# Later chunks convolved a step sooner and transposed by the DMA crossbar, no adds of x in the steps where chunks enter

## The chip, the cores and the metric

The kernel runs on one core of a Trainium2 chip. The metric is the device time of one execution in microseconds (us). A kernel was executed several times; the numbers below are medians with lowest and highest, and one execution of each kernel left a profile and a trace. Engines are called as the profile calls them: PE (tensor engine), DVE (vector), ACT (scalar), POOL (GpSimd), SP (sync); a "q" after the name (ACTq) is that engine's stream of DMA issues.

## The reference

A causal convolution of 7 taps over the sequence gives x; then a phase layer mixes tokens with two 4224x4224 matrices and channels with two 192x192 ones.

```python
def _attn_ref(x, weight):                  # x: 8 x 4224 x 192, weight: 8 heads x 7 taps
    w = softmax(weight)                    # (cut) over the taps, + 1e-9 in the divisor
    out = np.einsum('hk,bskhg->bshg', w, windows(x))        # causal, zero padded
    return out.reshape(B, S, D)

def _moe_ref(x, w_theta, w_tok_r, w_tok_i, w_ch):
    theta = x @ w_theta
    zr, zi = x * np.cos(theta), x * np.sin(theta)
    y = np.einsum('ts,bsd->btd', w_tok_r, zr) + np.einsum('ts,bsd->btd', w_tok_i, zi)
    u = x + y
    return u + np.maximum(u @ w_ch, 0.0)
```

Nearly all the work is the two token mixes, a product of 4224x4224 by 4224x1536 twice. The kernel does them by a scheme of seven products instead of eight for each pair of blocks.

## The kernel before

The 4224 tokens are cut into 33 **chunks** of 128. A chunk is loaded, convolved on PE, transposed, multiplied with w_theta, and turned into seven operands `z`. Eleven chunks fit in SBUF at a time. The output rows are 33 blocks, worked on in pairs: a **step** is one pair of row blocks against the chunks present, seven **runs** of up to 22 matmuls (a step with one block has four). After 17 steps a chunk has met all rows, and its place goes to the next. So there are 58 steps, and three kinds:

- **entering steps** 17 to 22 and 35 to 40, in which chunks 11 to 32 replace older ones, mostly two in a step;
- **quiet steps** 23 to 34, with eleven chunks and nothing else;
- **final steps** 41 to 57, which also compute the output; for it u is transposed by 24 DMA crossings.

```python
base = [0, 0, 1, 1, 2, 3, 3, 4, 4, 5, 5]
start = [base[k % NW] + (NU + 1) * (k // NW) for k in range(NK)]   # NW = 11, NU = 17
...
def crossed(uT, u):                                   # 128 x 1536, 384 KB, issued by ACT
    act(nc.scalar.dma_start(out=uT, in_=u, transpose=True))

def transposed(uT, u, by_dve=False):                  # 6 transposes on PE, then a copy
    tp = banks("tp", F16)
    for k in range(6):
        pe(nc.tensor.transpose(tp[:, 0, k * P : (k + 1) * P], u[:, k * P : (k + 1) * P], ident))
    evacuate(uT.rearrange("p k s -> p (k s)"), tp[:, 0, 0 : 6 * P], by_dve)
...
class Chunk:
    def conv(self, j):
        if j == 0:
            self.z = zpool.tile([P, 7, HN], F16, name="z", tag="z")
            self.x = self.z[:, T2 : T2 + 2, :].rearrange("p t n -> p (t n)")   # x lies inside z
        ...                                           # 8 matmuls, ACT copies; j == 1 writes xs
    def tasks(self):
        for j in range(2):
            yield lambda j=j: self.conv(j)
        for g in range(NG):
            yield lambda g=g: self.transpose(g)       # transposed(...), one half each
        for g in range(NG):
            yield lambda g=g: self.theta(g)
        ...                                           # products (DVE), differences (DVE)
```

Every row block must have x added once. An **add of x** is done in one of two ways. In most steps POOL adds `xr`, read back from DRAM, to the partial sums `pv`. For steps called `ahead`, x is added in DRAM by an accumulating DMA of two halves, some steps before the sums are read.

```python
visits = [v for v in range(NU, NSTEP) if v % NU == t % NU]
for i, tb in enumerate(self.tbs):
    at = [v for v in visits if self.known(tb) < v - 1 and v + NU < NSTEP]
    at = at[0] if at else visits[-1]
    if t == at:
        self.adds.append(i)
...
def add_x(self, i):
    if not self.ahead:
        xr = wk.tile([P, N], F16, name="xr", tag="xr", bufs=1)
        nc.sync.dma_start(out=xr, in_=xs[rows, :])
        pool(nc.gpsimd.tensor_tensor(out=self.pv[i], in0=self.pv[i], in1=xr, op=ALU.add))
        return
    for cols in (slice(0, HN), slice(HN, N)):
        pool(nc.gpsimd.dma_start(out=part[...][self.tbs[i], :, cols],
                                 in_=xs[rows, cols], accum_op=ALU.add))
```

Work is hung into a step by its position from 0 to 7: loads of weights two steps ahead, the turning of weights on DVE one step ahead, chunk loads at 4.5 of the step two before a chunk's start, everything else of a chunk from 0.1 on in the step before its start.

Of the kernel before, what the change touches and what calls it, by code (L numbers as in the profile page):

```python
# [16 lines left out]
def kernel(  # L17
# [91 lines left out]
    def banks(name, dtype=F32):  # L109
        return mmpool.tile([P, 2, PC if dtype == F32 else 2 * PC], dtype,  # L110
                           name=name, tag="mm")
# [20 lines left out]
    def channel_mix(tT, w):  # L132

        v = banks("v")
        for k in range(2):
            for b in range(2):
                for i in range(2):
                    pe(nc.tensor.matmul(  # L138
                        v[:, k, b * D : (b + 1) * D], lhsT=tT[:, 3 * k + b + i, :],
                        rhs=w[:, 2 * b + i, :], start=(i == 0), stop=(i == 1),  # L140
                    ))
        return v[:, :, 0 : 2 * D]
# [24 lines left out]
    class Chunk:  # L167
# [23 lines left out]

        def conv(self, j):

            if j == 0:
                self.z = zpool.tile([P, 7, HN], F16, name="z", tag="z")
                self.x = self.z[:, T2 : T2 + 2, :].rearrange("p t n -> p (t n)")
            pc = banks("pc")
            for h in range(4):
                for half in range(2):
                    pe(nc.tensor.matmul(  # L200
                        pc[half * 2 * Q : (half + 1) * 2 * Q, h // 2,
                           h % 2 * B * G : (h % 2 + 1) * B * G],
                        lhsT=bands[:, 4 * j + h, :, :].rearrange("p a m -> p (a m)"),
                        rhs=self.xw[:, half, :, (4 * j + h) * G : (4 * j + h + 1) * G],
                        start=True, stop=True,
                    ))
            evacuate(
                self.x.rearrange("p (b d) -> p b d", d=D)[
                    :, :, 4 * j * G : 4 * (j + 1) * G
                ].rearrange("p b (i h g) -> p i h b g", i=2, h=2),  # L210
                pc[:, :, 0 : 2 * B * G].rearrange("p i (h b g) -> p i h b g", h=2, b=B),
                self.k == 0 and j == 1,
            )
            if j == 1:
                for a in range(NQ):
                    t0 = token(self.k, a)
                    nc.sync.dma_start(
                        out=xs[t0 : t0 + Q, :], in_=self.x[a * Q : (a + 1) * Q, :]
                    )

        def transpose(self, g):
# [4 lines left out]
                0 < self.k < 3 or (self.k, g) == (0, 1),  # L226
            )

        def theta(self, g):
            v = channel_mix(self.xT[:, 6 * g : 6 * g + 6, :], wth).rearrange(  # L230
                "p k (b h e) -> p k b h e", b=2, h=2
            )
            for first, bias in ((Z11, half_pi[:]), (Z21, None)):
                o = self.z[:, first : first + 2, :].rearrange(
                    "p h (k b e) -> p k b h e", b=2, e=HD
                )[:, 2 * g : 2 * g + 2, :, :, :]
                args = dict(out=o, in_=v, func=AT.Sin)
                if bias is not None:
                    args.update(bias=bias, scale=1.0)
                act(nc.scalar.activation(**args))  # L240
# [14 lines left out]
        def tasks(self):  # L255

            for j in range(2):
                yield lambda j=j: self.conv(j)
            for g in range(NG):
                yield lambda g=g: self.transpose(g)  # L260
            for g in range(NG):
                yield lambda g=g: self.theta(g)
            yield lambda: self.product(Z11)
            yield lambda: self.product(Z21)
            yield lambda: self.sums(0)
            yield lambda: self.sums(1)
# [13 lines left out]
    class Step:  # L280


        def __init__(self, t):
            self.t, self.u, self.ks = t, unit(t), active(t)
            self.n = len(self.ks)
            self.tbs = [tb for tb in (2 * self.u, 2 * self.u + 1) if tb < NT]
            self.pair = len(self.tbs) == 2
            self.first = t < NU
            self.final = t + NU >= NSTEP
            self.late = self.final and self.n < NW  # L290
            self.ahead = self.late or 0 <= t + NU - NSTEP < 2
            visits = [v for v in range(NU, NSTEP) if v % NU == t % NU]
            self.adds = []
            for i, tb in enumerate(self.tbs):
                at = [v for v in visits if self.known(tb) < v - 1 and v + NU < NSTEP]
                at = at[0] if at else visits[-1]
                if t == at:
                    self.adds.append(i)
            self.time = 0.324 * self.n * (7 if self.pair else 4)
            self.st, self.w, self.ub, self.uT, self.pv = {}, {}, {}, {}, []  # L300
# [199 lines left out]
    def step_events(t):  # L500
        found = []
        s = steps[t]
        if t + 1 < NSTEP:
            found += steps[t + 1].w_tasks()
            found.append((1.6, steps[t + 1].load_rows))
            if not steps[t + 1].ahead:
                for i in steps[t + 1].adds:
                    found.append((3.3 + 1.7 * i, lambda i=i: steps[t + 1].add_x(i)))
        for s in steps[t:]:
            if s.ahead and t == s.t - (4 if s.late else 10):  # L510
                for i in s.adds:
                    found.append((3.3 + 1.7 * i, lambda s=s, i=i: s.add_x(i)))
        if t + 2 < NSTEP:
            nxt = steps[t + 2]
            for m in (1, 2):
                found.append((1.3 + 3 * (m - 1), lambda m=m: nxt.load_w(m)))
        for at, f in outputs:
            begin = at - sum(s.time for s in steps[:t])
            if 0 <= begin < steps[t].time:
                found.append((7 * begin / steps[t].time, f))  # L520
        if t >= NU - 2:
            new = [k for k in range(NK) if start[k] == t + 2 and k >= NW]
            for k in new:
                found.append((4.5, lambda k=k: load_chunk(k)))
            at = 0.1
            for k in (k for k in range(NK) if start[k] == t + 1 and k >= NW):
                pos = [0, .5, 1.3, 1.6, 2.1, 2.5, 3.1, 3.15, 3.4, 3.6]

                def add(at, j, k):
                    def go():  # L530
                        if j == 0:
                            chunks[k].todo = chunks[k].tasks()
                        next(chunks[k].todo)()
                    found.append((at, go))
                for j, p in enumerate(pos):
                    add(at + p, j, k)
                at += 2.3
        return found


# [185 lines left out]
```

## Time and profile before

| | before |
|---|---|
| time | 1475.88 us median of 3 (1469.09 to 1477.83), profiled execution 1468.28 |
| PE busy | 1418.6 of 1466.6 us, mean granted clock 0.999 |
| transposes of x on PE in later rounds | 44 groups of six, 0.33 us each |
| adds of x | 30 on POOL, 6 accumulating transfers |
| crossings | 24, all in final steps |

The page and the timeline are read in the prediction below. The page's DMA queues: each line gives packets, MB, and the time that the packets took as a share of what 16 engines have in the span; the crossings are queue 10.

```profile
q10 hardware_dynamic: 37632, 9.44, 3.8%
```

All instructions on the tile `uT` in the kernel before: for the issue of a crossing the shortest, median and longest time in ns, and in the last line the time from issue to landing in us.

```profile
L155 ACTq DMA_TRANSPOSE uT<-ub x24: 1290/1436/4943, 1065.0 to 1376.0; - x24
...
DMA to landing us min/median/max: 3.2/6.2/10.0
```

Last the DMA view of the first entering steps alone, 410 to 565 us: the two large queues, and of two transfers the KB and the median time to landing.

```profile
q0 software_dynamic: 22724, 10.49, 55.2%
q1 hardware_dynamic: 6320, 22.42, 41.3%
...
xs<-z SPq DMA_DIRECT2D x36, 96.0 KB, 4.0
st<-in_moe_w_tok_i_dram POOLq DMA_DIRECT2D x16, 144.0 KB, 4.7
```

A packet of a crossing is 9.44 MB / 37632 = 251 bytes on average, and 24 crossings took 3.8% x 1466.6 / 24 = 2.3 us of all engines each. And in the entering steps, where the change puts 22 more, the queues already stand at 55.2 + 41.3 = 97%, though nothing is late yet.

### The profile page before, as it was taken

Reading aid. Unit: us, or ns where it says so; the run is one execution under the profiler, and the core shown is the slowest. Engines: PE = TensorE matmul, PEld = TensorE weight load, DVE = VectorE, ACT = ScalarE, POOL = GpSimd, SP = SyncE. Lnnn points to the kernel's source line nnn. Section 1 sums busy time; section 2 is a strip of 40 time slices with the busy share of each in tenths; the row PEclk is TensorE's granted clock in tenths of the full one; section 3 lists DMA queues with packets and bytes.
Section 4 is the critical chain, followed back from the end, with each engine's and each line's share of the span. In section 5 each row is a group of like instructions: output and inputs, shape, how many; then the busy total and the mean of one; then the engine's idle time right before and its main releaser. Section 6 shows DMA issues by size and latency. Waiting matters only on the chain.

```text
span 1466.6 us, 23784 instructions
## 1 busy us (share of the span) xinstructions
PE 1418.6 (97%) x9807; PEld 887.2 (60%) x9807; DVE 1021.4 (70%) x1050; ACT 323.1 (22%) x413; POOL 444.7 (30%) x649
## 2 busy tenths in 40 slices
PE   7789999999999899999999999989999999999997
PEld 4556666666666466666656556656666666666665
DVE  6884554545548777866776767877878777767676
ACT  6861111111124145000000003434210010010034
POOL 7422211111233432341422442443224124213210
PEclk9999999999999999999999999999999999999999
DMA  9976756465699999987886899989979989999983
GB/s 172 219 174 147 139 98 151 89 150 97 138 232 213 201 259 222 242 221 188 196 222 148 240 162 217 254 198 228 241 165 219 206 198 219 200 216 204 213 208 123
DMA packets 271165, 279.63 MB, mean 191 GB/s; under 512 B 106576, under 2 KB 240080, under 8 KB 271056
## 3 DMA queue, kind: packets, MB, share of 16 engines
q0 software_dynamic: 160736, 87.43, 46.9%
q1 hardware_dynamic: 72688, 181.24, 35.5%
q10 hardware_dynamic: 37632, 9.44, 3.8%
q8 instruction: 77, 1.26, 0.3%
q14 instruction: 32, 0.26, 0.1%
HBM read 245.49 MB, written 103.42 MB: 238 GB/s over the span
## 4 chain that ended last, share of the span: by engine, by line
PE 84%; DVE 8%; ACT 3%; DMA 2%; issue 1%; POOL 1%; DVEq 0%; SPq 0%; ACTq 0%; POOLq 0%
PE y L426 76%; PE v L138 5%; DVE wt L338 2%; DVE pv L391 2%; ACT z L240 2%; PE pc L200 2%; PE tp L160 1%; DVE z L245 1%; DMA uT<-ub 1%; DVE z L251 1%; DVE wt L326 1%; ACT uT L148 1%; DVE pv L463 1%; ACT pv L389 0%; POOL pv L373 0%
## 5 line engine op out<-in xcount | busy, mean ns | idle before, releaser
L426 PE MATMUL y<-z,wt 128*128 128x384 f16 x7656 | 1290.1, 326 | 20.5 <-DVE pv L391 19.5
L426 PEld LDWEIGHTS <-wt 128*128 128x128 f16 x7656 | 739.9, 98 | 495.9 <-issue 22.1
L391 DVE TENSOR_TENSOR pv<-y,pv 128x768 f32<-128x768 f32 x324 | 308.4, 952 | 307.5 <-PE y L426 260.7
L326 DVE STREAM_TRANSPOSE wt<-st 128x1408 f16<-128x1408 f16 (+7 forms) x224 | 327.5, 1464 | 40.4 <-PE y L426 36.2
L313 POOL DMA_DIRECT2D st<-in_moe_w_tok_i_dram x232 | 132.5, 580 | 486.8 <-DVE wt L326 463.9
L313 POOL DMA_DIRECT2D st<-in_moe_w_tok_r_dram x232 | 132.7, 581 | 458.5 <-DVE wt L326 445.2
L338 DVE TENSOR_TENSOR wt<-wt 128x1408 f16<-128x1408 f16 (+7 forms) x216 | 219.4, 1016 | 45.6 <-PE y L426 43.4
L148 ACT ACTIVATE z<-pc 128x768 f16<-128x768 f32 x65 | 52.9, 813 | 400.5 <-PE pc L200 400.5
L448 ACT ACTIVATE ub<-pv 128x768 f16<-128x768 f32 x66 | 52.5, 835 | 342.4 <-DVE pv L391 337.3
L389 ACT ACTIVATE pv<-y 128x768 f32<-128x768 f32 x66 | 53.7, 813 | 282.7 <-PE y L426 282.7
L138 PEld LDWEIGHTS <-uT 128*128 128x128 f16 x1056 | 90.8, 98 | 25.9 <-issue 7.8
L373 POOL TENSOR_TENSOR pv<-pv,xr 128x1536 f32<-128x1536 f32 x30 | 94.5, 3151 | 15.5 <-issue 8.1
L187 POOL DMA_DIRECT2D xw<-in_x_dram x132 | 76.7, 596 | 25.8 <-issue 7.0
L463 DVE SCALAR_TENSOR_TENSOR pv<-v,pv 128x768 f32<-128x768 f32 x66 | 62.8, 954 | 22.4 <-PE v L138 20.2
L148 ACT ACTIVATE uT<-tp 128x768 f16<-128x768 f16 x79 | 63.0, 815 | 63.1 <-PE tp L160 62.2
L251 DVE TENSOR_TENSOR z<-z 128x768 f16<-128x768 f16 x132 | 73.3, 555 | 3.8
L245 DVE TENSOR_TENSOR z<-z 128x1536 f16<-128x1536 f16 x66 | 63.5, 997 | 9.0 <-ACT z L240 9.0
L240 ACT ACTIVATE z<-v,half_pi 128x768 f16<-128x768 f32 x66 | 59.6, 902 | 41.9 <-PE v L138 41.6
L138 PE MATMUL v<-wch,uT 128*128 128x192 f16 x528 | 54.3, 246 | 3.5 <-DMA uT<-ub 1.6
L138 PE MATMUL v<-wth,uT 128*128 128x192 f16 x528 | 54.3, 246 | 3.0 <-ACT z L240 2.8
L240 ACT ACTIVATE z<-v 128x768 f16<-128x768 f32 x66 | 53.1, 805 | 0.0
L160 PE MATMUL tp<-ident,z 128*128 128x128 f16 x396 | 33.4, 222 | 8.8 <-ACT z L240 8.3
(43 smaller groups left out, 139.2 us busy)
## 6 DMA issues: line engine op xcount, KB each, us to landing
part<-pv SPq DMA_DIRECT2D x79, 768.0 KB, 4.0
pv<-part SPq DMA_DIRECT2D x79, 768.0 KB, 5.5
out_dram<-pv SPq DMA_DIRECT2D x66, 384.0 KB, 4.6
st<-in_moe_w_tok_r_dram POOLq DMA_DIRECT2D x136, 176.0 KB, 5.5
st<-in_moe_w_tok_i_dram POOLq DMA_DIRECT2D x136, 176.0 KB, 4.8
xs<-z SPq DMA_DIRECT2D x132, 96.0 KB, 4.2
xw<-in_x_dram POOLq DMA_DIRECT2D x121, 96.0 KB, 5.8
xr<-xs SPq DMA_DIRECT2D x30, 384.0 KB, 4.5
```

The source lines that it names most:

```text
L138: pe(nc.tensor.matmul(v[:, k, b * D : (b + 1) * D], lhsT=tT[:, 3 * k + b + i, :], rhs=w[:, 2 * b + i, :], start=(i == 0), stop=(i == 1),))
L148: act(nc.scalar.activation(out=out, in_=in_, func=AT.Copy))
L240: act(nc.scalar.activation(**args))
L245: dve(nc.vector.tensor_tensor(out=o, in0=xv, in1=o, op=ALU.mult))
L251: dve(nc.vector.tensor_tensor(out=z[:, o, :], in0=z[:, a, :], in1=z[:, b, :], op=ALU.subtract))
L313: pool(nc.gpsimd.dma_start(out=st[a * Q : (a + 1) * Q, 0:nb, :, 0:n] .rearrange("i r bt s -> i (r bt) s"), in_=w[self.tbs[0] * P : (self.t ...
L326: dve(nc.vector.transpose(self.w[name][:, 0 : self.n, :, :], self.st[int(name[1])][:, int(name[0]) - 1, :, 0 : self.n * Q] .rearrange("p b ...
L338: dve(nc.vector.tensor_tensor(out=self.w[name][:, 0 : self.n, :, :], in0=self.w[a][:, 0 : self.n, :, :], in1=self.w[b][:, 0 : self.n, :, : ...
L373: pool(nc.gpsimd.tensor_tensor(out=self.pv[i], in0=self.pv[i], in1=xr, op=ALU.add))
L391: dve(nc.vector.tensor_tensor(out=o, in0=yv, in1=o, op=ALU.add))
L426: pe(nc.tensor.matmul(y[cn][:, q, 0:BH], lhsT=self.w[wn][:, c, :, :].rearrange("p bt i -> p (bt i)"), rhs=chunks[k].z[:, zn, q * BH : (q + ...
L463: dve(nc.vector.scalar_tensor_tensor(out=ub, in0=channel_mix(self.uT[i][:, 6 * g : 6 * g + 6, :], wch), scalar=0.0, in1=ub, op0=ALU.max, o ...
```

## The change

The intent is to give PE less to do. x of the later chunks is convolved a step sooner, into a buffer of its own (`ub`, which is free until the final steps), and transposed by the crossbar from there. And no add of x falls in an entering step, where POOL's add slows DVE.

```diff
         def conv(self, j):
-            if j == 0:
+            if j == 0 and self.k < NW:
                 self.z = zpool.tile([P, 7, HN], F16, name="z", tag="z")
                 self.x = self.z[:, T2 : T2 + 2, :].rearrange("p t n -> p (t n)")
+            elif j == 0:
+                self.x = wk.tile([P, N], F16, name="ub", tag="ub", bufs=2)[:, :]
...
+        def cross(self):
+            self.xT = turned()
+            crossed(self.xT, self.x)
+
         def theta(self, g):
+            if g == 0 and self.k >= NW:
+                self.z = zpool.tile([P, 7, HN], F16, name="z", tag="z")
...
-            for g in range(NG):
-                yield lambda g=g: self.transpose(g)
+            yield self.cross
...
-                at = [v for v in visits if self.known(tb) < v - 1 and v + NU < NSTEP]
+                at = [v for v in visits if self.known(tb) < v - 1 and v + NU < NSTEP
+                      and NU + 1 + base[-1] < v <= 2 * NU]
...
-                found.append((4.5, lambda k=k: load_chunk(k)))
...
-                pos = [0, .5, 1.3, 1.6, 2.1, 2.5, 3.1, 3.15, 3.4, 3.6]
...
+        for i, k in enumerate(entering(2)):
+            found.append((0.1 + 0.5 * i, lambda k=k: load_chunk(k)))
+            for at in (4.2, 4.6, 5.1):                       # conv 0, conv 1, cross
+                add(k, at + i)
+        for i, k in enumerate(entering(1)):
+            for at in (1.5, 1.9, 2.5, 2.55, 2.8, 3):         # theta 0, 1, products, differences
+                add(k, at + 1.7 * i)
```

The six adds that leave the entering steps are issued in steps 49 to 53 as accumulating transfers of two halves each: POOL adds go from 30 to 24, accumulating transfers from 6 to 18.

More of the change, by code (lines that the diff above doesn't have):

```diff
@@ L520, in step_events, with entering, add, go @@
                 found.append((7 * begin / steps[t].time, f))
-        if t >= NU - 2:
-            new = [k for k in range(NK) if start[k] == t + 2 and k >= NW]
-            for k in new:
-                found.append((4.5, lambda k=k: load_chunk(k)))
-            at = 0.1
-            for k in (k for k in range(NK) if start[k] == t + 1 and k >= NW):
-                pos = [0, .5, 1.3, 1.6, 2.1, 2.5, 3.1, 3.15, 3.4, 3.6]
-                def add(at, j, k):
-                    def go():
-                        if j == 0:
-                            chunks[k].todo = chunks[k].tasks()
-                        next(chunks[k].todo)()
-                    found.append((at, go))
-                for j, p in enumerate(pos):
-                    add(at + p, j, k)
-                at += 2.3
+        def entering(ahead):
+            return [k for k in range(NW, NK) if start[k] == t + ahead]
+        def add(k, at):
+            def go():
+                if "todo" not in vars(chunks[k]):
+                    chunks[k].todo = chunks[k].tasks()
+                next(chunks[k].todo)()
+            found.append((at, go))
+        for i, k in enumerate(entering(2)):
[5 more added lines that the diff above has]
+                add(k, at + 1.7 * i)
         return found
```

## The prediction

> **What bounds the kernel now.** I read the page's busy shares and chain, then the costliest groups, then what the tensor engine waited for, and last the timeline of the stretches where new chunks enter, since the change touches nothing else but the adds of x.
>
> ```profile
> PE 1418.6 (97%) x9807; PEld 887.2 (60%) x9807; DVE 1021.4 (70%) x1050; ACT 323.1 (22%) x413; POOL 444.7 (30%) x649
> PE 84%; DVE 8%; ACT 3%; DMA 2%; issue 1%; POOL 1%; DVEq 0%; SPq 0%; ACTq 0%; POOLq 0%
> L426 PE MATMUL y<-z,wt 128*128 128x384 f16 x7656 | 1290.1, 326 | 20.5 <-DVE pv L391 19.5
> L160 PE MATMUL tp<-ident,z 128*128 128x128 f16 x396 | 33.4, 222 | 8.8 <-ACT z L240 8.3
> L373 POOL TENSOR_TENSOR pv<-pv,xr 128x1536 f32<-128x1536 f32 x30 | 94.5, 3151 | 15.5 <-issue 8.1
> ```
>
> PE is the bound: 48 us of 1466.6 are not busy, so time falls only if PE gets less work or fewer waits. The work concerned is the transposes of x (396); the wait concerned is that for L391, the add that empties an accumulator bank on DVE (19.5 us).
>
> ```profile
> 427.17 2.45 PE L426 MATMUL y<-z,wt 128*128 128x384 f16 x14
> 429.46 0.50 PE L160 MATMUL tp<-ident,z 128*128 128x128 f16 x6
> 429.79 1.14 PE L426 MATMUL y<-z,wt 128*128 128x384 f16 x6
> ```
>
> The 0.50 us includes the pipeline's tail. What six transposes take from the stream is 429.46 to 429.79, 0.33 us.
>
> ```profile
> 473.62 5.04 DVE L245 TENSOR_TENSOR z<-z 128x1536 f16<-128x1536 f16 x2
> 474.72 3.12 POOL L373 TENSOR_TENSOR pv<-pv,xr 128x1536 f32<-128x1536 f32 x1
> 478.69 1.15 DVE L251 TENSOR_TENSOR z<-z 128x768 f16<-128x768 f16 x2
> 479.76 0.95 DVE L391 TENSOR_TENSOR pv<-y,pv 128x768 f32<-128x768 f32 x1
> 480.76 0.48 PE L426 MATMUL y<-z,wt 128*128 128x384 f16 x2 [3.12 <-DVE pv L391]
> ```
>
> Here lies the other half. Two products on DVE take 5.04 us beside an add of x on POOL; undisturbed, the same pair takes 1.82 (at 438.29). DVE falls 3.2 us behind, the bank is emptied late, and PE stands 3.12 us. In a step where chunks enter, DVE has nothing to catch up with.
>
> **What the Trainium skill says.** "TensorE: Matmul & The Clock Gate", section "Back-to-back issue gap", gives N/2.4 + 2.5 ns for a warm array: 162.5 ns at 384 columns, 55.8 at 128. The trace agrees: 38 matmuls in 6.34 us, less a tail of 0.33, are 0.1625 us each, and 6 x 55.8 is the 0.33 us above. The same page, "Why this matters for your kernels", warns of idle gaps over about 3 us: a half clock follows. The trace has one such case: after a wait of 2.81 us ended at 503.09, the mean granted clock from 503 to 507 is 0.57. The wait of 3.12 us at 480.76 had none, so a gap near 3 us may or may not cost this. "GPSIMD Engine Reference", section "1. Specifications", says that GpSimd's SBUF interfaces are shared with VectorE, with contention for instructions with two SBUF inputs; the 5.04 us above is that. "DMA: Bandwidth & Descriptors", section "Issuing engines are not separate DMA queues", says a DMA started by the scalar engine runs on the same 16 engines as all others, so the added crossings compete with the loads; whether that hurts is a rival below.
>
> **Part 1, transposes leave PE.** Chunks 11 to 32 are the 22 that enter later (two rounds of six steps, mostly two chunks a step). Each has two groups of six transposes: 44 groups x 0.33 = 14.7 us of PE time gone, all of it in a stretch where PE is full. ACT loses 44 copies of 0.81 us, which frees nothing, as ACT is 22% busy.
>
> **Part 2, no adds in entering steps.** By the old rule six of the 30 POOL adds fall in steps 19, 20, 38 and 39, by the new none. They are those at 474.72, 493.80, 508.04, 946.55, 964.92 and 980.26 on POOL. The PE waits for L391 behind them are 3.12 (480.76), 2.81 (503.09), 2.01 (958.68), 1.74 (987.91) and 0.57 (994.49): 10.25 us. The half clock after the second cost about 3.4 us x 1/2 = 1.7 more. Together 12 us.
>
> **Part 3, the work is in another order.** Loads and convolutions go a step ahead; theta, products and differences come earlier in their step and closer together. I counted DVE's work between two emptyings against PE's time for one run (9 chunks: 18 x 0.1626 = 2.93 us; plus 0.55 for a convolution half, 0.66 for a theta half). Durations are start-to-next-start spacings of 434 to 453 us: emptying 0.87, transpose of weights 1.29, weight sum 0.66, product pair 1.74, two differences 1.12. An emptying must be done when the next run ends. For the old order this gives 26.67 us for a step with two chunks and no wait; the trace shows 26.68 from one to the next (425.06 to 451.74). For the new order, times from the step's start:
> - PE: the runs end at 2.93, 6.52, 10.11, 14.36, 18.39, 22.42 and 25.35.
> - DVE: the emptying after run 3 ends at 15.4 to 16.4. Then a weight transpose, both products and all four differences of the second chunk stand in front of the next one: 1.29 + 1.74 + 2.24 + 0.87 = 6.1, so it ends near 22.6. It was due at 22.42. About 0.2 us of wait.
> - Steps followed by ten chunks (18 and 36), with only one chunk convolved in them, have 1.1 us less PE work there and dearer weights: 1.8 us of wait each. Step 22, with none convolved, 1.6.
> - Step 40 has one block of rows, so four runs (11.7 us + four thetas 2.64 = 14.35 of PE), but DVE must prepare weights of 11 chunks for step 41 (8 instructions, 9.4 us), two chunks' products and differences (8.0) and three or four emptyings: near 20 us. Before, PE had 17.9 us and waited 0.48 + 0.80; now it waits 4.9, and perhaps pays a half clock, 1 us on average.
>
> The sum of new waits: about 1 (five plain steps) + 3.6 + 1.6 + 4.9 + 1 = 12, less 1.3 that were there before: 10.8.
>
> **Part 4, the crossings and the late adds.** 22 crossings of 384 KB are added. A crossing is issued at 5.1 of 7 of a step and used at 1.5 of the next: 3.4/7 of 25.5 us, 12 us; the 24 of the old kernel land in 6.2 us (median), 10.0 at most. Hidden. The six adds of x move to the end as accumulating DMAs, up to four halves a step. The old kernel already has such a step with two more halves: 1365 to 1393 us, DMA share 1.13, PE busy all 28.00 us. Hidden too, but I put 1 us for it.
>
> **Sum:** -14.7 - 12 + 10.8 + 1 = -15. The three timings are 1469 to 1478 while the profiled execution took 1468; if the usual run loses a bit more to the waits that Part 2 removes, the gain is some 2 us larger: -17, 1475.9 to **1459 us**, 1.1%.
>
> **Rivals.**
> 1. *DVE does not become the limit.* If the emptyings keep up, Parts 1 and 2 count in full: -26.7 us, 1449. For it: DVE is 70% busy overall. Against it: in the entering steps it had no gaps (434 to 453 us: one after another), and PE's steps now shorten while DVE's work doesn't.
> 2. *DMA becomes the limit.* The windows of entering steps show DMA shares of 0.91 to 1.10. The old crossings are 3.8% of 1466.6 us for 24, so 2.3 us of all engines each; two a step are 0.18 more. If loads then come late, PE waits at the convolutions or at theta, and 10 to 20 us go: 1465 to 1480. Against it: the stretch of step 40 moved 297 GB/s at a share of 1.06, and entering steps now move some 200 to 250 and would add 31; loads of weights and x have over 10 us of slack.
> 3. *The adds' waits return elsewhere.* If the late accumulates delay the last steps' crossings (PE waited 1.02 us for one already), some 5 us come back: 1464.
>
> **Range and chances.** Parts 1 and 2 are read off; Part 3 is arithmetic that can be off by its own 10 us in either direction. Rival 1 (a quarter) gives the low end, rivals 2 and 3 (a fifth) the high end: 1447 to 1468. Faster by 2% needs 1446.4, beyond even rival 1 unless the usual run suffers more than the profiled one: 0.1. Slower by 2% needs a real DMA stall: 0.03.
>
> **What would show it.** Transposes out of z 132 instead of 396, and 22 crossings more; POOL adds 24; no wait of PE near 3 us in entering steps, but short ones for L391 in the last run of steps 18, 22 and 36, and one of 4 to 5 us at the first run after step 40, the largest of all; steps with two chunks 25.4 to 25.6 us instead of 26.7. Wrong would be: waits of PE for x's load or for a crossing in entering steps (rival 2), or no such wait after step 40 (rival 1).

## The result

| | before | after |
|---|---|---|
| time, median (lowest to highest) | 1472.55 us (1469.09 to 1477.83, 4 executions) | 1517.94 us (1512.04 to 1521.21, 4 executions) |
| profiled execution, span | 1466.6 us | 1518.6 us |
| mean granted clock of PE | 0.999 | 0.983 |

The ratio is 1.0301, with an interval of 1.0248 to 1.0353: **slower by 3.0%**, against a prediction of 1459. Ratios here and below are the mean time of one kernel's executions over that of the other's of the same rounds, so they are not quite the ratio of the medians. Executions over 1.5% slower than the fastest of the same kernel are left out of the means.

The page of the changed kernel: busy shares, the chain that ended last by engine, and two of its groups (busy us and mean ns after the bar, then PE's idle time before them and what ended it).

```profile
PE 1422.2 (94%) x9543; PEld 878.4 (58%) x9543; DVE 1017.6 (67%) x1050; ACT 289.2 (19%) x369; POOL 435.0 (29%) x655
...
PE 70%; DMA 17%; DVE 7%; ACT 4%; issue 2%; POOL 1%; SPq 0%; DVEq 0%; ACTq 0%; POOLq 0%
...
L381 POOL TENSOR_TENSOR pv<-pv,xr 128x1536 f32<-128x1536 f32 x24 | 74.9, 3119 | 8.5 <-DMA xr<-xs 8.2
L138 PE MATMUL v<-wth,uT 128*128 128x192 f16 x528 | 56.1, 251 | 22.0 <-DMA uT<-ub 19.5
```

PE has 264 matmuls fewer, as the change meant, and yet is busy 3.6 us longer, and idle 96.4 us where it was 48.0. DMA's share of the chain went from 2 to 17%. The busy time is the lower clock: 1418.6 less the 14.7 of the transposes is 1403.9, so some 18 us of busy time were stretched (an estimate from these two pages).

What PE waited for in the changed kernel, total, times and longest in us (before, the crossings cost 1.6 us and x's load nothing):

```profile
PE v L138 <- DMA uT<-ub: 31.3, 12, 9.1
PE y L434 <- DVE pv L399: 17.4, 16, 5.0
PE pc L202 <- DMA xw<-in_x_dram: 16.6, 5, 5.5
...
PE pc L202 <- DMA xw<-xw: 3.8, 5, 1.8
```

Crossings and the loads of x account for 51.7 us of waiting. The tile `uT` and the DMA view of the first entering steps (415 to 585 us), both of the changed kernel, say why:

```profile
L155 ACTq DMA_TRANSPOSE uT<-ub x46: 1290/2829/12697, 418.5 to 1427.3; - x46
...
DMA to landing us min/median/max: 3.2/9.7/23.5
```

```profile
q0 software_dynamic: 20736, 9.70, 49.5%
q1 hardware_dynamic: 6275, 22.62, 41.3%
q10 hardware_dynamic: 17248, 4.33, 21.6%
...
xs<-ub SPq DMA_DIRECT2D x44, 96.0 KB, 6.8
...
st<-in_moe_w_tok_i_dram POOLq DMA_DIRECT2D x16, 144.0 KB, 11.5
...
uT<-ub ACTq DMA_TRANSPOSE x11, 12.8
```

The three queues now stand at 112%. A load of 144 KB of weights lands in 11.5 us where it took 4.7 (the other matrix's: 11.5 after 8.1), a write of xs in 6.8 instead of 4.0, and a crossing in 12.8 us (median), more than the 12 us of room. Each crossing of this window took 21.6% x 170 / 11 = 3.3 us of all engines, not 2.3.

The timeline has the waits themselves (start, length, and in brackets the wait before it):

```profile
954.12 4.24 ACTq L155 DMA_TRANSPOSE uT<-ub  x1
```

```profile
603.82 2.44 PE L434 MATMUL y<-z,wt 128*128 128x384 f16 x14 [1.69 <-DVE pv L399]
...
972.23 1.46 PE L138 MATMUL v<-wth,uT 128*128 128x192 f16 x8 [6.50 <-DMA uT<-ub]
...
1077.59 4.64 PE L434 MATMUL y<-z,wt 128*128 128x384 f16 x14 [4.95 <-DVE pv L399]
...
1402.84 1.46 PE L138 MATMUL v<-wch,uT 128*128 128x192 f16 x8 [9.14 <-DMA uT<-ub]
```

The crossing issued at 954.12 was needed at 965.7 and came at 972.2. Of the two waits for DVE at 603.82 and 1077.59 the prediction had named the place and nearly the size. The last line is in step 52, a final step that the change did not touch except for the adds of x; the issue of its crossing had held ACT for 12.70 us.

The steps can be cut out of each trace at the first token matmul of a step. This table of stretches, in us, is what the experiments are read with (each entering stretch with the step beside it into which its work reaches):

| kernel (profiled execution) | steps 16-22, entering | 23-33, quiet | 34-41, entering | 42-56, final |
|---|---|---|---|---|
| before | 192.2 | 267.4 | 207.1 | 382.4 |
| after | 206.9 | 268.3 | 230.1 | 395.0 |
| difference | +14.7 | +0.9 | +23.0 | +12.6 |
| transposes on PE again | 190.3 | 268.3 | 211.9 | 386.0 |
| before, new adds only | 185.2 | 268.4 | 203.2 | 402.9 |
| before, adds moved to quiet steps | 185.2 | 266.5 | 203.2 | 386.6 |
| before, idle crossings in entering steps | 210.0 | 268.4 | 236.7 | 387.6 |
| before, idle crossings in quiet steps, paced | 191.9 | 273.8 | 208.8 | 398.0 |

The loss is in the entering steps (37.7 us) and the final steps (12.6); of the latter, 11.3 us are step 52 alone.

### The profile page after: what moved, and what is told of

Same layout as the page of the kernel before. It is cut to its first block, busy times and chain, and to the rows that moved or that the text cites. A ratio compares the mean times of both kernels' runs of the same rounds, so it can differ in the third digit from the quotient of the medians.

```text
span 1518.6 us, 23255 instructions
## 1 busy us (share of the span) xinstructions
PE 1422.2 (94%) x9543; PEld 878.4 (58%) x9543; DVE 1017.6 (67%) x1050; ACT 289.2 (19%) x369; POOL 435.0 (29%) x655
## 4 chain that ended last, share of the span: by engine, by line
PE 70%; DMA 17%; DVE 7%; ACT 4%; issue 2%; POOL 1%; SPq 0%; DVEq 0%; ACTq 0%; POOLq 0%
PE y L434 63%; DMA uT<-ub 11%; PE v L138 4%; DMA xw<-in_x_dram 2%; DVE wt L346 2%; DMA xw<-xw 2%; ACT z L248 1%; DVE pv L399 1%; DVE wt L334 1%; PE pc L202 1%; DVE z L253 1%; DVE z L259 1%; POOL xw L187 1%; DVE pv L471 1%; ACT ub L148 1%
## 5 line engine op out<-in xcount | busy, mean ns | idle before, releaser
L148 ACT ACTIVATE ub<-pc 128x768 f16<-128x768 f32 x44 | 35.3, 810 | 391.8 <-PE pc L202 364.4
L381 POOL TENSOR_TENSOR pv<-pv,xr 128x1536 f32<-128x1536 f32 x24 | 74.9, 3119 | 8.5 <-DMA xr<-xs 8.2
L138 PE MATMUL v<-wth,uT 128*128 128x192 f16 x528 | 56.1, 251 | 22.0 <-DMA uT<-ub 19.5
L202 PE MATMUL pc<-xw,bands 96*64 96x192 f16 x528 | 38.7, 264 | 23.8 <-DMA xw<-in_x_dram 16.6
L202 PEld LDWEIGHTS <-bands 96*64 96x64 f16 x528 | 23.0, 114 | 46.2 <-issue 29.3
L253 DVE TENSOR_TENSOR z<-ub,z 128x1536 f16<-128x1536 f16 x44 | 39.3, 933 | 1.3 <-ACT z L248 1.3
```

The costliest lines, as they stand in the source:

```text
L138: pe(nc.tensor.matmul(v[:, k, b * D : (b + 1) * D], lhsT=tT[:, 3 * k + b + i, :], rhs=w[:, 2 * b + i, :], start=(i == 0), stop=(i == 1),))
L202: pe(nc.tensor.matmul(pc[half * 2 * Q : (half + 1) * 2 * Q, h // 2, h % 2 * B * G : (h % 2 + 1) * B * G], lhsT=bands[:, 4 * j + h, :, :].r ...
```

## The experiments

The theories at the start: **A**, the crossings of x overload the DMA engines of the entering steps; **B**, the new order of loads and convolutions is what makes x late; **C**, the late accumulating transfers hold up the final steps. Later the question became what in a crossing costs the time. All kernels gave correct results. All are compared with executions of the kernel before on the same chip in the same rounds, whose medians were 1469 to 1471 us.

### The changed kernel with the transposes on PE again

```diff
-            yield self.cross
+            yield lambda: [self.transpose(g) for g in range(NG)]
```

> The changed kernel with x of the later chunks transposed on PE again (two groups of six and two copies by ACT), at the place in the order where the crossing was issued; buffers, early loads and convolutions, and the rule for the adds stay. Theory A, the crossings are too slow for the DMA queues of the entering steps and hold up the loads queued with them: PE's 19.5 us of waits for uT before theta vanish, the 23 us of waits for x's loads (xw) fall below 5, PE gets 14.7 us of transposes back; total 1475 to 1490 us (the wait of 9 us in step 52 stays). Theory B, x's loads come late because of their new place in the order of buffers, whatever the crossings do: the waits for xw stay near 20 us, total 1500 to 1512 us.

Measured: 1491.34 us median (1475.38 to 1494.24), ratio 1.0121 (1.0062 to 1.0179). In the trace no wait for a crossing and none for x's load is left in the entering steps; they take 402.2 us instead of 437.0. The order of loads and convolutions was the changed one, so B falls as the cause of the late x: with the same order and no crossings of x, x is in time. The crossings cost 34.8 us in the entering steps of the profiled executions. The profiled execution was the fastest of four and lacks the stop of step 52; the other three were 13 to 19 us longer and left no trace.

### Old rule of adds in the changed kernel, new rule alone in the kernel before

```diff
 e2: changed kernel              -   and NU + 1 + base[-1] < v <= 2 * NU]
 e3: kernel before               +   and NU + 1 + base[-1] < v <= 2 * NU]
```

> The changed kernel with the old rule for the adds of x: 30 adds on POOL, six of them in entering steps, and 6 accumulating DMAs at the end instead of 18. Theory: the wait of 9.1 us for a crossing in step 52, with the half clock after it, is due to the added accumulates: it vanishes, and steps 49 to 53 are 12 us shorter. In the entering steps the adds stall DVE again by some 3 us each, but part of that hides in the waits for DMA: total 1508 to 1518 us. Rival: the crossing in step 52 is late for another reason, and the total is 1520 us or more.

> The kernel before with the new rule for the adds of x and nothing else. As predicted, PE's waits of 10.25 us in steps 18, 19, 20, 37 and 38 and the half clock vanish (12 us). If the late accumulates alone delay a crossing in step 52, 12 us come back there and the total is that of before within 5 us; if they don't, without the other parts, it is 1458 to 1464 us.

Measured: with the old rule 1496.0 us (1492.23 to 1507.4), 1.0188 (1.0141 to 1.0234); the new rule alone 1478.36 (1472.85 to 1480.13), 1.0048 (1.002 to 1.0077). PE's waits with the new rule alone:

```profile
PE v L138 <- DMA uT<-ub: 18.8, 9, 10.5
PE y L427 <- DVE pv L392: 11.3, 12, 1.8
```

The wait for DVE falls from 19.5 to 11.3, and both entering stretches together get 10.9 us shorter, as predicted. But a wait for a crossing appears at the end, and step 52 takes 42.7 us instead of 27.7. With the old rule step 52 takes 27.7 us, though step 53 there has a wait of 6.5; the total lies below both ranges expected. In the changed kernel the new rule thus cost 16.4 us in all (means of +44.3 and +27.9 against the kernel before). So C holds for step 52: the stop comes with the rule of adds and without any crossing of x. Over all traces of this case, this stop is in five of the six with the adds issued four steps ahead in steps 49 to 53 (step 52 takes 39.0 to 46.2 us; the sixth is the one above with 27.7), and in none of the others (27.7 to 29.1). How an accumulating transfer delays a crossing was not examined.

### Chunks loaded still sooner

```diff
+        for i, k in enumerate(entering(3)):
+            found.append((5.0 + 0.5 * i, lambda k=k: load_chunk(k)))
         for i, k in enumerate(entering(2)):
-            found.append((0.1 + 0.5 * i, lambda k=k: load_chunk(k)))
```

> The changed kernel with x's loads put 2.1 of 7 of a step sooner into the order of the program (5.0 of the step ahead instead of 0.1 of the step in which they are convolved), same six buffers. Theory B (order of buffers): the loads take buffers sooner, the 23 us of PE waits for xw fall under 8, total 1490 to 1500 us. Theory A (queues full because of the crossings): the waits move to uT or stay, total 1510 to 1525 us.

Measured: 1573.11 us (1548.86 to 1578.93), two of the four slow, so no ratio is given; the profiled one, fast, took 1568.72, above both ranges expected. No wait for x is left, but this one in its place:

```profile
PE v L138 <- DMA uT<-ub: 97.2, 17, 15.4
```

The edit changed the order of the program, but not when the loads start. A load of x takes one of six buffers that the partial sums use as well, and the trace shows that it is issued when one comes free: counted in steps and fractions of a step, the first loads of the 22 chunks were issued at 27.42 in the mean in the changed kernel and at 27.44 here. So this run does not test more lead, and why the crossings wait so much longer in it stays open. The same look shows how x came to be late in the changed kernel. This is what POOL waited for before it could issue such loads, in the changed kernel:

```profile
POOL xw L187 <- DMA part<-pv: 67.1, 7, 19.1
```

and in the one with the transposes on PE again:

```profile
POOL xw L187 <- DMA part<-pv: 34.4, 4, 11.3
```

Beside crossings the write-backs of the sums (`part<-pv`) land in 7.2 us instead of 4.9 (medians of 415 to 585 us in these two kernels) and buffers come free later. The loads of the five chunks that PE waited for ended their issue 3.2 to 10.2 us before they were needed, and took 9.8 to 11.5 us to land; with the transposes on PE the same five had 12.4 to 16.9 us.

### Crossings that nobody reads, beside a plain copy of the same bytes

The kernel before, with each later chunk's x also crossed into an unused `ub` buffer; then with a plain copy there; then with the crossing issued by SP.

```diff
+                if self.k >= NW:
+                    dummy = wk.tile([P, N], F16, name="ub", tag="ub", bufs=2)
+                    crossed(dummy[:, :].rearrange("p (k s) -> p k s", s=P), self.x)      # idle crossing
+                    # or act(nc.scalar.dma_start(out=dummy, in_=self.x))                 # idle copy
+                    # or nc.sync.dma_start(out=..., in_=self.x, transpose=True)          # issued by SP
```

> The kernel before, with its PE transposes and its old order, and one crossing more per later chunk (22), of x into a buffer that stands empty in those steps and that nobody reads. If a crossing as such overloads the DMA queues of the entering steps (theory A), loads there land later by half or more (median of the weights' loads 8 us or more instead of 5 to 8) and PE waits for loads or emptyings by 10 to 25 us: total 1480 to 1495 us. If a crossing only hurts where theta waits for it (rival), nothing in the old order waits: 1468 to 1474 us.

> The same with a plain copy of the same 384 KB from x into that buffer, issued by the same queue at the same place, in place of the crossing. If it is the crossing's small packets (some 1568 of 256 bytes each) that take the engines' time, the copy costs under a third of what the crossing does: 1468 to 1476 us. If the bytes, or one DMA more in the queues' order, are the cost, it is the same as with the crossing.

> The kernel before with the 22 idle crossings, issued by SP's queue instead of ACT's. In the run with ACT most of PE's waits were for ACT's copies of transposes (35.5 us), behind crossings whose issue held ACT for 1.4 to 8.7 us. If that holding is the whole cost, these waits vanish and the total is 1472 to 1485 us. If the load on the DMA engines is the cost, SP's queue is held instead, loads of x and of partial sums come late, and the total is 1490 us or more.

| | median (range) | ratio (interval) |
|---|---|---|
| 22 idle crossings, by ACT | 1524.06 (1518.94 to 1529.14) | 1.0371 (1.033 to 1.0411) |
| 22 idle copies of the same 384 KB, by ACT | 1474.24 (1470.9 to 1479.24) | 1.003 (1.0 to 1.0059) |
| 22 idle crossings, by SP | 1501.95 (1498.07 to 1512.87) | 1.0206 (1.0165 to 1.0248) |

So it is not the bytes: the copies are nearly free, the crossings of the same bytes cost more than the whole change lost. The issues of the idle transfers, first as crossings, then as copies, ns:

```profile
L155 ACTq DMA_TRANSPOSE ub<-z x22: 1386/3160/8725, 428.2 to 1073.3; - x22
```

```profile
L222 ACTq DMA_DIRECT2D ub<-z x22: 472/472/517, 428.1 to 1039.0; - x22
```

A copy holds ACT 0.47 us; a crossing holds it 1.39 to 8.73. Beside this the engines: 22 crossings raise queue 10's time from 3.8% of 1466.6 us (55.7) to 9.1% of 1520.0 (138.3), 3.8 us each; 22 copies raise it to 5.6% of 1477.5 (82.7), 1.2 us each. What the held ACT does to PE is the first wait of the kernel with crossings, and the timeline shows one case:

```profile
PE v L138 <- ACT uT L148: 35.5, 13, 10.8
```

```profile
962.76 5.09 ACTq L155 DMA_TRANSPOSE ub<-z  x1
967.90 1.51 ACT L148 ACTIVATE uT<-tp 128x768 f16<-128x768 f16 x2 [5.17 <-PE y L429]
```

ACT's copies of PE's transposes start only when the issue is over, and PE stands for want of them, 0.91 us here. Not all of the 35.5 us is the holding: before the longest wait, 10.8 us in step 38, the issue took 3.2 us, and ACT had stood 11.1 us in front of it, until the crossing before had landed. Issued by SP instead, the wait for ACT is gone, and somewhat under half of the cost with it. What stays are waits for DVE (26.9 us, of which the kernel before has 19.5) and for x's loads (14.5): the load on the DMA engines, though SP was itself held by the issues, 1.43 to 9.36 us each, and this run does not separate the two. So a crossing costs by what it takes of the engines and by how long it keeps the engine that issues it. Whether the small packets make it dear was not tested: no copy in such packets was run.

### Theta a little later

```diff
-            for at in (1.5, 1.9, 2.5, 2.55, 2.8, 3):
+            for at in (2.2, 2.6, 3.2, 3.25, 3.5, 3.7):
```

> The changed kernel with theta, products and differences 0.7 of 7 of a step later (2.2 to 3.7 instead of 1.5 to 3), so that a crossing has 15 us instead of 12. If only the room was too small for crossings that land after 12.8 us (median of the entering steps), the 19.5 us of PE waits for them fall under 6, and the total is 1495 to 1505 us. If the queues are over their capacity, late loads take the place of the crossings: waits for xw grow beyond their 23 us and the total stays 1510 to 1525 us. The wait of 5 us after step 40 stays either way or falls a little.

Measured: 1516.49 us (1508.16 to 1526.07), 1.0316 (1.0262 to 1.037): no gain. With more room the waits for crossings in the entering steps fell from 19.5 to 8.6 us (the other 15.5 of the 24.1 are in the final steps), but the waits for x grew to 14.4 and 9.7 us (loads and history copies), and the entering steps took 433.3 us instead of 437.0. So room for the crossings alone does not help. The wait after step 40 fell from 5.0 to 2.8.

### The accumulating transfers seven steps ahead instead of four

```diff
 (kernel before, new rule of adds)
-            if s.ahead and t == s.t - (4 if s.late else 10):
+            if s.ahead and t == s.t - (7 if s.late else 10):
```

> The kernel before with the new rule for the adds, and the accumulating DMAs of the last steps issued seven steps ahead instead of four, so that they fall into steps 46 to 50 and none into step 52. If the 15 us of step 52 in the run with the adds alone come from accumulates close together with that step's loads, they vanish and the 11 us of the entering steps remain: 1457 to 1464 us, faster than the kernel before by 0.5 to 0.8%. If they come from the number of accumulates wherever they are, some other step shows a wait of 5 us or more and the total is 1468 to 1480 us.

Measured: 1489.38 us (1482.06 to 1500.72, 6 executions), 1.0138 (1.009 to 1.0187). This is above both ranges expected. Step 52 is whole again (27.7 us), and steps 48, 49 and 50 have waits for crossings of 14.8, 5.3 and 11.4 us in all:

```profile
PE v L138 <- DMA uT<-ub: 32.5, 5, 11.4
```

The stop travels with the accumulating transfers, which is the strongest evidence for C: at both places tried among the final steps, a crossing of u is late.

### Half of x crossed, half transposed on PE

```diff
-            crossed(self.xT, self.x)
+            crossed(self.xT[:, 0:6, :], self.x[:, 0:GC])
+            transposed(self.xT[:, 6:12, :], self.x[:, GC:N])
```

> The changed kernel with half of each chunk's x crossed and half transposed on PE. If the crossings' share of the DMA engines (21.6% in the entering steps, 113% in all) is the cause, half of it (to some 103%) takes away much more than half of the waits: PE's waits for uT in entering steps 19.5 -> under 7 us, for xw 23 -> under 10; total 1485 to 1500 us. If every crossing costs a fixed amount, whatever its size, the total stays 1508 to 1520 us.

Measured: 1487.94 us (1483.18 to 1497.98), 1.0108 (1.0067 to 1.015). In the entering steps there is no wait for a crossing (they land in 7.4 us at the median of 415 to 585 us, where the three queues stand at 108%), and they take 186.4 and 209.4 us, 41 us less than with whole crossings and 6 less than with none. Half the crossings do far less than half the harm. The stop in step 52 stays (46.2 us instead of 27.7), and with it the loss.

### The adds moved to quiet steps

The kernel before, with the rule that no add falls in an entering step, and with steps 36 to 38 also done `ahead`, ten steps before, so that their adds are accumulating transfers in the quiet steps 26 to 28.

```diff
-            self.ahead = self.late or 0 <= t + NU - NSTEP < 2
+            self.ahead = self.late or 0 <= t + NU - NSTEP < 2 or 2 <= t - 2 * NU < 5
...
-                at = [v for v in visits if self.known(tb) < v - 1 and v + NU < NSTEP]
+                at = [v for v in visits if self.known(tb) < v - 1 and v + NU < NSTEP
+                      and v > NU + 1 + base[-1]]
```

> The kernel before, with five of the six adds of x that fell into entering steps done as accumulating DMAs in the quiet steps 26 to 28 instead of at the end (the sixth stays in step 39). Theory: the stalls of DVE beside POOL go (9 of the 11 us), and in quiet steps no crossing and no convolution waits behind the accumulates: 1458 to 1463 us, faster than the kernel before by 0.4 to 0.8%. If accumulates stop the engines wherever they are, steps 26 to 29 show waits of 5 us or more: 1468 to 1480 us.

Measured: **1461.61 us** (1458.66 to 1472.81, 6 executions), ratio 0.9932 (0.9895 to 0.997). The wait for DVE is down and the final steps are nearly as before:

```profile
PE y L427 <- DVE pv L392: 10.3, 12, 1.8
...
PE v L138 <- DMA uT<-ub: 3.6, 2, 3.2
```

This beats both kernels, by a little under 1%. It differs from "new rule alone" in where the moved adds go, and in the one of six that was not moved, and the means of the two are 1463.1 and 1477.4: the late place cost 14 us (17.0, each against the kernel before in its own rounds).

### Idle crossings in the quiet steps, unpaced and paced

Is a crossing dear by itself, or only where the engines are near full? First the kernel before with 22 idle crossings of a finished chunk, two in each of steps 23 to 33; then, since this was flawed, 22 of the weights just turned (352 KB), so that each must wait for its turn on DVE.

```diff
+        if 23 <= t < 34:                                     # paced form
+            def idle_crossing(name):
+                dummy = wk.tile([P, N], F16, name="ub", tag="ub", bufs=2)
+                crossed(dummy[:, 0 : NW * P].rearrange("p (k s) -> p k s", s=P),
+                        steps[t + 1].w[name].rearrange("p c bt i -> p (c bt i)"))
+            found.append((1.0, lambda: idle_crossing("11")))
+            found.append((5.0, lambda: idle_crossing("12")))
```

> The kernel before with 22 idle crossings of the same size in the eleven quiet steps 23 to 33, two a step, where the DMA engines are 86% busy and x is neither loaded nor convolved. If a crossing costs only where the engines are full already, PE waits no longer than before there (steps of 25.0 to 26.0 us, crossings land in 4 to 8 us): 1468 to 1474 us. If a crossing costs PE time anywhere, these steps lengthen by 1 us or more each: 1480 us or more.

> The kernel before, with 22 crossings of 352 KB that nobody reads (from the freshly turned weights, two in each of the quiet steps 23 to 33, so that each waits for its turn on VectorE and they cannot run back to back). Theory 'a crossing costs only where the 16 engines are full': the quiet steps have a DMA share near 0.9 or less, so the crossings land in 6 to 8 us and cost at most 8 us: under 1480 us, with no PE wait above 3 us in steps 23 to 33. Rival 'each crossing by itself costs about 2.4 us wherever it lies': 22 of them cost some 50 us, near 1520 us, as the same number did in the entering steps and in the unpaced burst.

Measured, unpaced: 1529.31 us (1521.96 to 1536.99), 1.0381 (1.0339 to 1.0422). The expectation was met in size for a reason that makes it worthless: the source was finished and ACT has almost nothing to do in quiet steps, so the crossings ran back to back:

```profile
586.64 120.11 ACTq L155 DMA_TRANSPOSE ub<-z  x21
```

PE stood 48.7 us in steps 24 and 25, the rest of the quiet steps being undisturbed. It says only that a burst of crossings stops everything else.

Measured, paced: 1494.18 us (1487.02 to 1574.72, the highest slow), 1.0127 (1.0068 to 1.0185). The quiet steps took 273.8 us instead of 267.4, so 22 crossings cost 6.4 us, of which one wait in step 25 is 4.6. The same number in the entering steps cost 210.0 + 236.7 - 192.2 - 207.1 = 47.4. That refutes a fixed price of 2.4 us a crossing. But the theory that the engines' share decides is not confirmed either. The DMA view of the quiet steps in this run, 590 to 850 us:

```profile
q0 software_dynamic: 22457, 14.88, 44.7%
q1 hardware_dynamic: 7617, 36.97, 41.3%
q10 hardware_dynamic: 30240, 7.57, 27.0%
...
ub<-wt ACTq DMA_TRANSPOSE x21, 7.7
```

The sum is 113%, as in the entering steps of the changed kernel (112%), and yet the crossings land in 7.7 us, not 12.8, and PE hardly waits. So the share alone is a poor criterion. What the quiet steps lack is work with a near deadline behind the crossings: no load of x, no copy on ACT that PE needs soon, no use of the crossing itself. Nor did an issue hold ACT for as long: 1.68 us at the median and 3.88 at most, against 3.16 and 8.73 for the unread crossings of the entering steps (which are of 384 KB and not 352). These are arguments from what differs, not a test of it. The rest of this run's loss, 15.6 us in the final steps, is in code that was not changed at all: step 53 had a wait of 9.4 us for a crossing of u. The final steps can lose so much by chance or by a shift in time; which, stays open.

### Half crossing and adds in quiet steps together

```diff
 (half of x crossed, as above)
+            self.ahead = ... or 2 <= t - 2 * NU < 5
-                      and NU + 1 + base[-1] < v <= 2 * NU]
+                      and v > NU + 1 + base[-1]]
```

> The changed kernel with half of x crossed and half transposed by PE, and with the adds of x in steps 36 to 38 done as accumulating transfers ten steps ahead, in quiet steps 26 to 28, and none in steps 49 to 53 beyond the old kernel's. Theory 'the loss is the sum of crossings in full steps and of late accumulates': entering steps 186 and 210 us as in the half-crossing run, final steps as in the kernel before: 1466 to 1475 us, and no wait of 5 us or more for a crossing in steps 49 to 53. Rival 'the end is slower by something else of the change (order of loads, own buffer for x)': step 52 keeps some 12 us more, and the time stays near 1485.

Measured: 1476.15 us (1468.91 to 1482.32), ratio 1.0021 (0.9971 to 1.0072). The mean is 13.4 us below that of the half crossing with late adds (1475.9 and 1489.3), the same step as between the two runs without crossings. The entering steps took 187.2 and 209.9, as expected. But the expectation of no large wait in the final steps failed for the profiled execution, the slowest of the four, with 10.4 us in step 48 and 4.4 in step 53:

```profile
PE v L138 <- DMA uT<-ub: 15.4, 4, 10.4
```

The fastest execution, 1468.91, can hardly hold such waits. By the means the parts add up to within a few us; what stopped the profiled execution in steps 48 and 53, with no late add, is not known. The change, mended in both places, is level with the kernel before, and the simpler version with the adds alone is ahead of it.

## Why the prediction was wrong

The means of the executions, each against the kernel before in the same rounds, give the change as a chain of single edits:

| edit | predicted | measured | from |
|---|---|---|---|
| adds out of the entering steps, at best in quiet ones (five of the six) | -12 | -9.6 | 1463.1 against 1472.7 |
| the moved adds late instead (Part 4) | +1 | +17.0 | new rule alone, +7.4, less -9.6 |
| new order of loads, convolution, theta (Part 3) | +10.8 | +10.6 | transposes on PE again, +18.0, less +7.4 |
| crossings in place of PE transposes (Parts 1 and 4) | -14.7 | +26.3 | changed kernel, +44.3, less +18.0 |
| sum | -15 | +44.3 | |

In the profiled traces the crossings cost 34.8 us in the entering steps alone; the means give less, as three of the four executions with PE transposes were longer than the traced one. The differences are between separate sets of executions; by the intervals above, a line is good to some 6 us (the first) to 12 (the fourth).

**Part 1 was right as arithmetic and lost its effect.** The 264 transposes left PE, and no step of its working is at fault; what took their place was dearer (Part 4). One thing about its source: the section of the Trainium skill that the prediction cites, "TensorE: Matmul & The Clock Gate", "Back-to-back issue gap", gives N/2.4 + 2.5 ns as the gap of an isolated matmul, and some 81 ns at 128 columns for a stream with weight loads. Here six transposes in 0.33 us are 55 ns each within a stream, so the trace sides with the formula. With only half of them gone, the entering steps were 6 us shorter than with all of them on PE, so part of this gain can be had.

**Part 2 was right.** The waits named are gone with the rule alone, and the entering steps are 10.9 us shorter against the predicted 12.

**Part 3 was right.** The waits for DVE stand where they were put: 1.69 us after the runs of step 22 (predicted 1.6), 4.95 after step 40 (predicted 4.9). The 1.8 us named for steps 18 and 36 are not there in the changed kernel (0.0 and 0.5), where PE waited for transfers in these steps and DVE could catch up. With the transposes on PE again, and no such waits, all four are there: 1.45 in step 18, 1.70 in step 22, 1.45 in step 36 and 5.28 after step 40. The sum is close to the prediction too, 10.6 us by the means (the entering steps of the traces give 402.2 - 388.4 = 13.8), and Rival 1, that DVE keeps up, is refuted.

**Part 4 failed, and with it the prediction.** Its step was: "used at 1.5 of the next: 3.4/7 of 25.5 us, 12 us; the 24 of the old kernel land in 6.2 us (median), 10.0 at most. Hidden." The landing times were taken from the final steps and carried over to the entering steps, whose queues already stood at 97%; there the crossings landed in 12.8 us at the median. Three things were missed. The crossings did not only arrive late, they made others late. The loads of x, which had "over 10 us of slack", cost 20.4 us of waits: they wait for buffers that late write-backs hold, and five were issued only 3.2 to 10.2 us before their use. The price of a crossing was 3.3 us of all engines there, not 2.3. And the issue itself holds ACT, 1.3 us at best and up to 12.7, which the working does not mention; with unread crossings somewhat under half of the cost went when SP issued them.

**"Hidden too, but I put 1 us for it"** was the second miss. The old kernel's busy stretch with two more halves had no wait, and the prediction took one such case as proof. Rival 3 named the right mechanism, late accumulates delaying crossings of u, at 5 us. It is 14 us to 17. In the final steps a crossing of u has no time to spare either, and when it is late PE stands up to 15 us in one step.

**Rival 2 was the right one** and was given 10 to 20 us; the chance for slower, 0.03, was far too small: rivals 2 and 3 came true together.

**The clock** was the third term. The working allowed one half clock, 1 us. The mean granted clock fell from 0.999 to 0.983, which is up to 0.016 x 1518.6 = 24 us of full-speed time, part of it inside the waits themselves. Behind each of the four waits of more than 4 us in that trace (4.95, 5.45, 6.50 and 9.14) the mean granted clock of the next 4 us was 0.50 to 0.53; of the four between 3 and 4 us one had this (0.59) and three did not (1.00). So a long wait must be entered at more than its length.

**What stays open.** Which deadline in the entering steps is decisive where the share of the engines is the same as in the paced quiet steps. How late accumulates delay a crossing. And why the final steps lose 5 to 19 us in some executions even with no late add, as in the paced run; only one execution of each kernel has a trace.

## What to carry to other kernels

Before moving work from a full engine to DMA, read landing times and queue shares in the very window where the new transfers will run, ask which short-deadline transfers will stand behind them, and test it with an unread copy of the new transfer in the old kernel: here that cost a few added lines and showed a loss no smaller than the real one. When one part of a change moves work elsewhere, look at what its new place is tight on: the adds gained some 10 us when moved to quiet steps, and moved to the end they lost this and 7 us more. And a partial move can take most of the gain: crossings of half the size cost nothing that could be seen in the entering steps.

## What the Trainium skill lacked or had wrong

- "DMA: Bandwidth & Descriptors", section "Latency and other measured facts", gives a DMA transpose 261 GB/s, 350 to 400 where contiguous. Here, by the time that its packets took of all engines: 9.44 MB in 3.8% of 1466.6 us, 169 GB/s, in the final steps of the kernel before; 4.33 MB in 21.6% of 170 us, 118 GB/s, beside the loads of the entering steps. Other transfers ran beside them in both, so neither is the rate of a crossing alone. A plain copy of the same tile, by the same measure, was 320 GB/s (384 KB in 1.2 us).
- The same page, section "Issuing engines are not separate DMA queues", is borne out in its main point: with crossings on ACT's queue, weights on POOL's queue landed in 11.5 us instead of 4.7. But it calls the time that it takes to initiate a DMA "usually small relative to the DMA itself". For the crossings of the changed kernel it was 1.29 us at least, 2.83 median and 12.70 at most, against a median of 9.7 to landing, and work behind it on ACT waited; a plain copy of the same size took 0.47.
- The page gives no measure of how near to full is too near. The sum of the queues' shares, 112 and 113% in two stretches, did not decide it: 22 crossings cost 47 us in the one kind of stretch (there 114%, with unread crossings) and 6 us in the other.
